# Order of the block products in a row step, packed weights split over two banks at once, and a buffer of its own for the last output block

## The chip, the cores and the metric

The kernel runs on one core of a Trainium2 chip. The metric is the device time of one execution in microseconds (us); a kernel's number is the median of its runs. One further execution was recorded by the hardware profiler, and its times stand in the rows below, counted from the start of its span. PE is TensorE's matmul, PEld its weight load, DVE is VectorE, ACT ScalarE, POOL GpSimd, and SP issues the DMAs.

## The reference, cut to what matters

```python
def reference(q, k, v, p, moe_*, moe2_*):       # B, H, S, D = 8, 8, 576, 64; 32 packed queries
    pp  = softmax(p k^T / 8) v                   # packed attention, per batch and head
    x   = softmax(q pp^T / 8) pp                 # unpacked again: 4608 tokens x 512
    xn  = x / sqrt(mean(x * x) + 1e-6) * rms_g
    y   = (silu(xn w_gate) * (xn w_val)) w_out   # 512 -> 1536 -> 512
    return ((y w1) * (y w2)) w3 w_out2           # 512 -> 1024 -> 1024 -> 512
```

## The kernel before

Each factor of a matrix product is split into a rounded high part and the rest (`split`, line 58: ACT copies to the high part, then an engine subtracts, nearly always DVE, for the low part), and three products (high high, high low, low high) stand for one in full precision.

**Attention and gated layer** (to about 524 us). For batch `b`, `wb_unit(b, g)` (line 335) multiplies the batch's packed values into one sixth `g` of the gate and value weights: 16 small matmuls on PE (line 342) fill a tile `t` of 128 x 2 x 512 that covers two PSUM banks. It is then split into `wbh` and `wbl`, by one ACT and one DVE instruction for each half `e`, four in all; there are 48 such units. `dense_units(b)` (line 367) runs the dense work: groups of six matmuls of 288 columns fill one of four banks (`gv`), first the gate group, which ACT (tanh, line 387, tile `th`) and DVE (line 388) read, then the value group, which ACT reads (line 392, tile `vl`). In a group the order is (wbh, ah), (wbh, al), (wbl, ah), so the low part is first needed by the fifth matmul. `wb_unit` for the next sixth is issued when four groups of the present one are left. The pieces of the attention of later batches are issued between the groups, at places written out by hand, and each engine works through its queue in program order.

**Down projection and weight folding** (to about 862 us). `group` (line 612) also lays out the seven combinations of w1 and w2 for the last part, in the order `ORDER` (line 595).

**Bilinear layers** (from 862 us to the end). Tokens come in five pairs of strips, three pairs of 512 columns and two of 384 (called wide and narrow below). `run(p)` (line 937) makes eight row steps and then a last layer. The products go by a scheme with seven block products for eight. `step(p, n)` (line 863) does the seven products of one row: each is six matmuls, into four banks `ta`, `tb`, `tc_`, `td`, which alternate between two sets from step to step. Before the change the order on PE is 0, 5, 4, 1, 6, 3, 2. Into `ta` go products 0 and then 1, into `tb` 5 and then 6, into `tc_` 4 and then 2, into `td` 3. The second product of a bank is added on top of the first, so it has to wait for whoever still reads the first: ACT reads product 0 (`p1`), DVE reads 5 for `u2`, DVE reads 6 for `u3`, then 4 for `c22`, which needs `u3`. Then DVE makes `s1`, from `td` and `u3`, multiplies it by `ta`, and adds `tc_` to `u2`; POOL does the rest. `u2` and `c22` are the two halves of a tile `uc` with two buffers, `p1` and `u3` come from a tile `hr` with five. The weights come by DMA in two units a step (products at positions 0 to 2, and 3 to 6), through four buffers.

The **last layer** runs 168 matmuls (line 973). `u3` (block 1, 0) and `c22` (block 1, 1) are stored from where they are; block (0, 1) is written over `u2` in `uc` and stored from there. The stores go out on SP's queue, one after each quarter of a product, and what is left at the end of the pass (line 1007).

Of the kernel before, what the change touches and what calls it, by code (L numbers as in the profile page):

```python
# [32 lines left out]
def packed_attention_swiglu_bilinear(ctx: ExitStack, tc, qT, kT, v, pT, rms_g, w_gv, w_out,  # L33
                                     w1, w2, w3T, w_out2, out):
    nc = tc.nc
# [16 lines left out]
    def slot(tag):  # L52
        return slots.tile([128, 2, 512], F32, tag=tag, name=tag, bufs=2)
# [4 lines left out]
    def split(hi, lo, src, eng_lo):  # L58
        nc.scalar.activation(out=hi, in_=src, func=AF.Copy)  # L59
        eng_lo.tensor_tensor(out=lo, in0=src, in1=hi.bitcast(F32), op=ALU.subtract)  # L60
# [274 lines left out]
    def wb_unit(b, g):  # L335
        gP1T = res["gP1T", b]
        while not all((g, c) in converted for c in range(NC)):
            next(gvw)
        t = slot("at")
        for c in range(NC):  # L340
            for e in range(2):
                nc.tensor.matmul(t[32 * c:32 * c + 32, e, :], lhsT=gP1T[64 * e:64 * e + 64, c, :],  # L342
                                 rhs=wgv[64 * e:64 * e + 64, c, :, 256 * g:256 * g + 256],
                                 start=True, stop=True, tile_position=(64 * e, 32 * c), skip_group_check=True)
        hi = dp.tile([128, 2, 512], F32R, tag="wbh", name="wbh", bufs=2)
        lo = dp.tile([128, 2, 512], F32R, tag="wbl", name="wbl", bufs=2)
        for e in range(2):
            split(hi[:, e], lo[:, e], t[:, e], nc.vector)
        wb[b, g] = (hi, lo)


# [56 lines left out]
    def drain(gen):  # L408
        for _ in gen:
            pass  # L410
# [36 lines left out]
    def wb_first():  # L447
        wb_unit(0, 0)
        yield
# [17 lines left out]
    for n in range(16):  # L467
        r, c = GROUPS[n // 4]
        w, kk = ((w1, r), (w1, r + 2), (w2, r), (w2, r + 2))[n % 4]
# [122 lines left out]

    ORDER = (0, 5, 4, 1, 6, 3, 2)
    parts = []

    def fetch_part(n):
# [13 lines left out]
    def group(g):  # L612
# [5 lines left out]
        def put(j, src, eng):  # L618
            hi, lo = (to[:, :, ORDER.index(j), s, :] for s in range(2))
            split(hi, lo, src.rearrange("p (i n) -> p i n", i=4), eng)  # L620
# [153 lines left out]
    def next_w():  # L774
        w = ws.pop(0)
        load_w()
        return w

    def width(p):
        return pairs[p][1]  # L780
# [5 lines left out]
    def diff(out, a, b, eng=None):  # L786
        (eng or nc.vector).tensor_tensor(out=out, in0=a, in1=b, op=ALU.subtract)
# [57 lines left out]
    def banks(n):  # L845
        if n % 2:
            return [pt.tile([128, 512], F32, tag="at", name="at", bufs=4) for _ in range(4)]
        return four("gv")
# [5 lines left out]
    def tmp():  # L854
        return rot.tile([128, TT], F32, tag="hr", name="hr", bufs=5)

    def two():
        return yp.tile([128, 2, TT], F32, tag="y", name="uc", bufs=2)

    def dve(out, a, b, op=ALU.add):  # L860
        nc.vector.tensor_tensor(out=out, in0=a, in1=b, op=op)  # L861

    def step(p, n):
        w = width(p)
        i = LAYER[n]
        half, k = divmod(i, 4)
        xh, xl = xs[p]

        def side(name):
            return sides[name][:, k, :w]  # L870

        def prod(t, j, start):
            pos = ORDER.index(j)
            wi, pos, n = (wa, pos, 3) if pos < 3 else (wb_, pos - 3, 4)
            wi = wi[:, :512 * n].rearrange("p (r j s n) -> p r j s n", r=2, j=n, s=2)
            at = 0
            for a, x in ((0, xh), (1, xh), (0, xl)):
                for r in range(2):
                    nc.tensor.matmul(t, lhsT=wi[:, r, pos, a], rhs=x[:, j, r, :w],  # L879
                                     start=(start and at == 0), stop=(at == 5), skip_group_check=True)  # L880
                    at += 1

        ta, tb, tc_, td = (t[:, :w] for t in banks(n))
        p1, u3, uc = tmp()[:, :w], tmp()[:, :w], two()
        u2, c22 = uc[:, 0, :w], uc[:, 1, :w]
        s1, s2 = (side("s21"), side("s22")) if half else (side("s11"), side("s12"))
        wa = next_w()
        prod(ta, 0, True)
        nc.scalar.activation(out=p1, in_=ta, func=AF.Copy)
        prod(tb, 5, True)  # L890
        dve(u2, tb, p1)
        prod(tc_, 4, True)
        yield
        wb_ = next_w()
        prod(ta, 1, False)
        prod(tb, 6, False)
        dve(u3, tb, p1)
        dve(c22, tc_, u3)
        yield
        prod(td, 3, True)  # L900
        dve(s1, td, u3)
        dve(s1, s1, ta, ALU.mult)
        prod(tc_, 2, False)
        dve(u2, tc_, u2)
        nc.gpsimd.tensor_tensor(out=s2, in0=u2, in1=c22, op=ALU.mult)  # L905
        if half == 0:
            diff(side("t1s"), s2, s1, nc.gpsimd)
        else:
            diff(side("t2s"), s2, side("t1s"), nc.gpsimd)
            diff(side("s12"), s2, side("s12"), nc.gpsimd)  # L910
            diff(side("t4s"), s1, side("t2s"), nc.gpsimd)
        yield
# [24 lines left out]
    def run(p):  # L937
        w = width(p)
        ahead = splitting(p, AHEAD)
        diffs = early(p + 1)  # L940
        for n in range(8):
            for part, _ in enumerate(step(p, n)):
                if part in EARLY.get(n, ()):
                    next(ahead)
                if n == 1 and part == 0:
                    fetch_y(p + 1)
                if n in (4, 5) and part == 1:
                    next(diffs, None)
        xs.pop(p)
        drain(ahead)  # L950
        drain(diffs)
        later = splitting(p, LATER)
        sum_ = sums(p + 1)
        acc = [[t[:, :w] for t in banks(m)] for m in range(2)]
        p1, u2, u3, c22 = [], [], [], []
        out_stores = []

        def keep(m, half, side, o):
            out_stores.append(dict(out=out[256 * half + 128 * m:256 * half + 128 * m + 128,
                                           pairs[p][0] + side * w:pairs[p][0] + side * w + w], in_=o))  # L960

        BANK = {0: 0, 1: 0, 5: 1, 6: 1, 4: 2, 2: 2, 3: 3}
        for a, j in enumerate(PROD):
            wi = next_w().rearrange("p (s i n) -> p s i n", s=2, i=4)
            last = {0: 1, 5: 6, 4: 2}.get(j, j) == j
            for k in range(4):
                for _ in range(ISSUE[4 * a + k]):
                    next(later, None)
                hi, lo = his.pop((j, k))
                for m in range(2):  # L970
                    t = acc[m][BANK[j]]
                    for n, (s, x) in enumerate(((0, hi), (1, hi), (0, lo))):
                        nc.tensor.matmul(t, lhsT=wi[:, s, k, 128 * m:128 * m + 128], rhs=x,  # L973
                                         start=(j in (0, 5, 4, 3) and k == 0 and n == 0),
                                         stop=(k == 3 and n == 2), skip_group_check=True)
                if k == 1:
                    next(sum_, None)
                if out_stores:
                    nc.sync.dma_start(**out_stores.pop(0))
            for m in range(2):  # L980
                ta, tb, tc_, td = acc[m]
                if j == 0:
                    p1.append(tmp()[:, :w])
                    nc.scalar.activation(out=p1[m], in_=ta, func=AF.Copy)
                elif j == 5:
                    uc = two()
                    u2.append(uc[:, 0, :w])
                    c22.append(uc[:, 1, :w])
                    dve(u2[m], tb, p1[m])
                elif j == 1:  # L990
                    c11 = tmp()[:, :w]
                    nc.scalar.activation(out=c11, in_=ta, func=AF.Copy)
                    keep(m, 0, 0, c11)
                elif j == 6:
                    u3.append(tmp()[:, :w])
                    dve(u3[m], tb, p1[m])
                    dve(c22[m], tc_, u3[m])
                    keep(m, 1, 1, c22[m])
                elif j == 3:
                    dve(u3[m], td, u3[m])  # L1000
                    keep(m, 1, 0, u3[m])
                elif j == 2:
                    dve(u2[m], tc_, u2[m])
                    keep(m, 0, 1, u2[m])
        drain(sum_)
        for x in out_stores:
            nc.sync.dma_start(**x)

    for p in range(len(pairs)):
        run(p)  # L1010
# [31 lines left out]
```

## Time and profile before

| | |
|---|---|
| time, median of 3 runs | 1409.88 us (1409.6 to 1412.5) |
| the profiled execution: its own time, and the span in the profile | 1410.05 us, 1408.3 us |
| busy over the span | PE 95%, PEld 79%, DVE 61%, POOL 43%, ACT 41% |
| PE on the chain that ended last | 79% (DVE 10%) |

The chain is followed back from the last instruction, at each step to what released it. A busy PE counts every matmul, also one that runs at a lower granted clock. An idle engine only costs time where the chain passes through it.

### The profile page before, as it was taken

How to read it: one execution, taken by the hardware profiler on the slowest of the kernel's cores; microseconds unless marked ns; L12 is line 12 of the kernel's file. 1: busy time of each engine (PE TensorE's matmuls, PEld its weight loads, DVE VectorE, ACT ScalarE, POOL GpSimd, SP SyncE). 2: the span in 40 equal slices, each digit the busy share in tenths (PEclk: the TensorE clock that was granted, in tenths of full speed). 3: DMA queues.
4: the chain of work that ended last, by engine and by line, in shares of the span. 5: the costliest groups of instructions: out<-in, count | busy, mean ns of one | idle time of the engine just before them, and what ended most of it. 6: DMA issues, size and time to landing. Idle time of an engine off the chain costs nothing.

```text
span 1408.3 us, 23274 instructions
## 1 busy us (share of the span) xinstructions
PE 1339.0 (95%) x8800; PEld 1119.5 (79%) x8800; DVE 857.2 (61%) x1356; ACT 573.7 (41%) x1141; POOL 606.5 (43%) x524
## 2 busy tenths in 40 slices
PE   4579999999999999999999999999999999999998
PEld 2358888788787888888878888778777777899998
DVE  4787776866767556745376564566458357457445
ACT  2455555655655665634243342024015103304113
POOL 2455456465555562312132212446345534535533
PEclk9699999999999999999999999999999999999999
DMA  9763566554542357743299875556655745777775
GB/s 315 280 216 89 214 203 211 186 178 146 175 142 106 128 167 246 266 154 121 83 341 375 341 265 210 214 196 226 256 194 190 275 178 209 244 278 254 265 257 181
DMA packets 86688, 301.94 MB, mean 214 GB/s; under 512 B 9520, under 2 KB 14640, under 8 KB 72624
## 3 DMA queue, kind: packets, MB, share of 16 engines
q1 hardware_dynamic: 86576, 300.46, 61.6%
q8 instruction: 69, 1.13, 0.4%
q14 instruction: 43, 0.35, 0.1%
HBM read 223.87 MB, written 76.55 MB: 213 GB/s over the span
## 4 chain that ended last, share of the span: by engine, by line
PE 79%; DVE 10%; ACT 2%; issue 2%; DMA 1%; POOL 1%; SPq 0%; ACTq 0%; DVEq 0%; POOLq 0%
PE gv L381 17%; PE at L568 12%; PE gv L879 11%; PE at L879 11%; PE gv L568 7%; PE gv L973 6%; PE at L973 6%; PE gv L669 3%; PE at L342 3%; DVE uc L861 2%; DVE hr L861 2%; PE at L297 1%; DVE th L388 1%; DVE c_t L115 1%; DVE wbl L60 1%
## 5 line engine op out<-in xcount | busy, mean ns | idle before, releaser
L393 POOL TENSOR_TENSOR ht<-th,vl 128x288 f32<-128x288 f32 x192 | 162.1, 854 | 118.7 <-ACT vl L392 61.6
L381 PE MATMUL gv<-ah,wbh 128*128 128x288 f32 x768 | 178.3, 313 | 15.8 <-ACT vl L392 11.1
L381 PEld LDWEIGHTS gv<-ah,wbh 128*128 128x128 f32 x768 | 122.0, 190 | 67.8 <-issue 22.8
L381 PE MATMUL gv<-al,wbh 128*128 128x288 f32 x768 | 166.7, 298 | 0.0
L381 PE MATMUL gv<-ah,wbl 128*128 128x288 f32 x768 | 164.7, 296 | 0.0
L905 POOL TENSOR_TENSOR s<-uc 128x512 f32<-128x512 f32 (+1 forms) x40 | 48.9, 1223 | 238.8 <-DVE uc L861 238.8
L60 DVE TENSOR_TENSOR hl<-hr,hh 128x512 fp32r<-128x512 f32 x108 | 99.4, 926 | 77.8 <-ACT hh L59 77.8
L118 POOL TENSOR_TENSOR c_o<-c_o,c_y 128x512 int32<-128x512 int32 x52 | 70.7, 1360 | 172.1 <-DVE c_o L116 111.3
L879 PE MATMUL gv<-xh,w 128*128 128x512 f32 (+1 forms) x560 | 140.6, 372 | 3.4 <-DVE uc L861 2.8
L879 PE MATMUL at<-xh,w 128*128 128x512 f32 (+1 forms) x560 | 140.4, 372 | 3.4 <-DVE uc L861 2.5
L381 PEld LDWEIGHTS gv<-al,wbh 128*128 128x128 f32 x768 | 124.4, 190 | 1.1 <-DVE al L60 1.1
L381 PEld LDWEIGHTS gv<-ah,wbl 128*128 128x128 f32 x768 | 124.2, 189 | 0.0
L879 PEld LDWEIGHTS gv<-xh,w 128*128 128x128 f32 x560 | 101.3, 188 | 24.0 <-DVE uc L861 11.3
L879 PEld LDWEIGHTS at<-xh,w 128*128 128x128 f32 x560 | 101.3, 188 | 23.6 <-DVE uc L861 11.0
L388 DVE SCALAR_TENSOR_TENSOR th<-th,gv 128x288 f32<-128x288 f32 x192 | 84.9, 445 | 50.6 <-ACT th L387 47.1
L59 ACT ACTIVATE hh<-hr 128x512 fp32r<-128x512 f32 x108 | 67.7, 629 | 117.2 <-PE at L568 58.5
L568 PE MATMUL at<-hh,wo_l 128*128 128x512 f32 x288 | 112.1, 389 | 0.0
L568 PE MATMUL at<-hh,wo_h 128*128 128x512 f32 x288 | 112.1, 389 | 0.0
L568 PE MATMUL at<-hl,wo_h 128*128 128x512 f32 x288 | 112.1, 389 | 0.0
L392 ACT ACTIVATE vl<-gv 128x288 f32<-128x288 f32 x192 | 80.0, 417 | 57.6 <-PE gv L381 53.0
L60 DVE TENSOR_TENSOR wbl<-at,wbh 128x512 fp32r<-128x512 f32 x96 | 65.8, 686 | 60.9 <-ACT wbh L59 60.3
L387 ACT ACTIVATE th<-gv 128x288 f32<-128x288 f32 x192 | 79.6, 415 | 35.9 <-PE gv L381 35.8
(154 smaller groups left out, 2815.4 us busy)
## 6 DMA issues: line engine op xcount, KB each, us to landing
w<-ws_d SPq DMA_DIRECT2D x40, 1024.0 KB, 5.0
w<-w_d SPq DMA_DIRECT2D x35, 1024.0 KB, 4.8
w<-ws_d SPq DMA_DIRECT2D x40, 768.0 KB, 5.1
hT_d<-ht SPq DMA_DIRECT2D x96, 288.0 KB, 3.3
hr<-hT_d SPq DMA_DIRECT2D x108, 256.0 KB, 4.6
w<-in_w_gv_dram SPq DMA_DIRECT2D x24, 512.0 KB, 7.0
w<-in_w_out_dram SPq DMA_DIRECT2D x20, 512.0 KB, 4.2
v<-in_v_dram SPq DMA_DIRECT2D x8, 1152.0 KB, 8.1
```

Source lines behind the costliest of these rows:

```text
L59: nc.scalar.activation(out=hi, in_=src, func=AF.Copy)
L60: eng_lo.tensor_tensor(out=lo, in0=src, in1=hi.bitcast(F32), op=ALU.subtract)
L118: nc.gpsimd.tensor_tensor(out=d, in0=d, in1=shape(y), op=ALU.add)
L381: nc.tensor.matmul(t[:, :HALF], lhsT=w[:, e, 256 * i + 128 * f:256 * i + 128 * f + 128], rhs=x[:, e, HALF * hf:HALF * hf + HALF], start=(n ...
L387: nc.scalar.activation(out=th, in_=t[:, :HALF], func=AF.Tanh, scale=0.5)
L388: nc.vector.scalar_tensor_tensor(out=th, in0=th, scalar=1.0, in1=t[:, :HALF], op0=ALU.add, op1=ALU.mult)
L392: nc.scalar.activation(out=vl, in_=t[:, :HALF], func=AF.Copy, scale=0.5)
L393: nc.gpsimd.tensor_tensor(out=ht[:, hf], in0=th, in1=vl, op=ALU.mult)
L568: nc.tensor.matmul(acc[m], lhsT=w[:, kk, 128 * m:128 * m + 128], rhs=x, start=(kk == 0 and a == 0), stop=(kk == NF - 1 and a == 2))
L861: nc.vector.tensor_tensor(out=out, in0=a, in1=b, op=op)
L879: nc.tensor.matmul(t, lhsT=wi[:, r, pos, a], rhs=x[:, j, r, :w], start=(start and at == 0), stop=(at == 5), skip_group_check=True)
L973: nc.tensor.matmul(t, lhsT=wi[:, s, k, 128 * m:128 * m + 128], rhs=x, start=(j in (0, 5, 4, 3) and k == 0 and n == 0), stop=(k == 3 and n ...
```

## The change

Three edits.

- In `step`, product 6 comes before product 1 on PE, and the weights lie in that order (`ORDER`). The order on DVE stays u2, u3, c22, s1, s1, u2.
- In `wb_unit` the tile of two banks is split by one ACT instruction and one DVE instruction of 1024 elements a partition each, where there were two of 512 on either engine.
- In the last layer block (0, 1) is written to a buffer of the tile `hr` and stored from there, no longer from `u2`'s half of `uc`.

```diff
@@ wb_unit
         lo = dp.tile([128, 2, 512], F32R, tag="wbl", name="wbl", bufs=2)
-        for e in range(2):
-            split(hi[:, e], lo[:, e], t[:, e], nc.vector)
+        split(hi, lo, t, nc.vector)
@@
-    ORDER = (0, 5, 4, 1, 6, 3, 2)
+    ORDER = (0, 5, 4, 6, 1, 3, 2)
@@ step
         wb_ = next_w()
-        prod(ta, 1, False)
         prod(tb, 6, False)
         dve(u3, tb, p1)
         dve(c22, tc_, u3)
+        prod(ta, 1, False)
         yield
@@ run, last layer
                 elif j == 2:
-                    dve(u2[m], tc_, u2[m])
-                    keep(m, 0, 1, u2[m])
+                    c12 = tmp()[:, :w]
+                    dve(c12, tc_, u2[m])
+                    keep(m, 0, 1, c12)
```

## Rows read from the trace of the kernel before

**Rows 1.** The page, part 1: busy us (share of the span) x instructions.

```profile
PE 1339.0 (95%) x8800; PEld 1119.5 (79%) x8800; DVE 857.2 (61%) x1356; ACT 573.7 (41%) x1141; POOL 606.5 (43%) x524
```

**Rows 2.** Busy time by stretch: us, PE, PEld, DVE, ACT, POOL, granted clock, DMA.

```profile
0.00:110.00 110.00, 63.17 (x666) 43.37 (x667) 77.51 (x138) 50.05 (x99) 46.68 (x49) 0.83 0.75 262
110.00:475.00 365.00, 353.86 (x3736) 296.79 (x3734) 256.91 (x512) 210.53 (x493) 201.13 (x220) 1.00 0.49 163
475.00:524.00 49.00, 49.00 (x403) 43.09 (x396) 27.05 (x48) 33.26 (x79) 30.76 (x32) 1.00 0.52 165
524.00:862.40 338.40, 337.51 (x1488) 278.88 (x1487) 195.98 (x241) 145.25 (x241) 79.63 (x48) 1.00 0.67 236
862.40:942.40 80.00, 78.80 (x338) 62.46 (x337) 40.13 (x56) 9.34 (x16) 29.33 (x21) 1.00 0.64 230
1220.30:1282.50 62.20, 60.61 (x338) 58.06 (x337) 30.26 (x56) 6.41 (x14) 21.05 (x20) 1.00 0.80 283
```

**Rows 3.** The chain in order of time, one wide row step: start us, us, what.

```profile
882.50 6.83 PE gv L879 x30
...
890.08 0.70 DVE uc L861
...
890.83 1.67 PE gv L879 x6
892.50 0.69 PE at L879 x3
```

**Rows 4.** The chain in order of time, one narrow row step.

```profile
1266.98 5.22 PE gv L879 x30
...
1274.77 1.39 PE at L879 x8
```

**Rows 5.** Timeline of DVE, u2 of a wide and two narrow steps [idle before, releaser].

```profile
885.38 0.69 DVE L861 TENSOR_TENSOR uc<-gv,hr 128x512 f32<-128x512 f32 x1 [2.15 <-PE gv L879]
...
1269.21 0.56 DVE L861 TENSOR_TENSOR uc<-gv,hr 128x384 f32<-128x384 f32 x1 [1.21 <-POOL s L905]
...
1277.34 0.56 DVE L861 TENSOR_TENSOR uc<-at,hr 128x384 f32<-128x384 f32 x1 [1.97 <-ACT sh L59]
```

**Rows 6.** Timeline of SP and DVE around the start of the last pass.

```profile
1308.42 0.95 SPq L979 DMA_DIRECT2D out_dram<-hr  x2
...
1316.14 0.56 DVE L861 TENSOR_TENSOR uc<-gv,hr 128x384 f32<-128x384 f32 x1 [3.00 <-DMA out_dram<-uc]
```

**Rows 7.** Waits, 110 to 475 us: total us, times, longest us.

```profile
ACT wbh L59 <- DVE wbl L60: 40.1, 38, 2.3
...
PE gv L381 <- ACT vl L392: 10.9, 8, 2.1
```

**Rows 8.** Groups by line, 110 to 524 us: busy us, mean ns of one, idle before.

```profile
L388 DVE SCALAR_TENSOR_TENSOR th<-th,gv 128x288 f32<-128x288 f32 x180 | 79.7, 446 | 49.2 <-ACT th L387 45.8 <-POOL ht L393 2.3 <-POOL rinv L315 0.8
L387 ACT ACTIVATE th<-gv 128x288 f32<-128x288 f32 x179 | 74.2, 415 | 35.6 <-PE gv L381 35.5
L60 DVE TENSOR_TENSOR wbl<-at,wbh 128x512 fp32r<-128x512 f32 x88 | 60.4, 686 | 58.2 <-ACT wbh L59 57.6
L59 ACT ACTIVATE wbh<-at 128x512 fp32r<-128x512 f32 x88 | 52.7, 599 | 61.2 <-DVE wbl L60 45.1 <-PE at L342 15.9
```

**Rows 9.** Timelines of ACT, DVE and PE, one stall of the gated layer.

```profile
209.30 0.64 ACT L59 ACTIVATE wbh<-at 128x512 fp32r<-128x512 f32 x1
212.25 0.60 ACT L59 ACTIVATE wbh<-at 128x512 fp32r<-128x512 f32 x1 [2.31 <-DVE wbl L60]
...
211.59 0.63 DVE L60 TENSOR_TENSOR wbl<-at,wbh 128x512 fp32r<-128x512 f32 x1
212.88 0.69 DVE L60 TENSOR_TENSOR wbl<-at,wbh 128x512 fp32r<-128x512 f32 x1 [0.66 <-ACT wbh L59]
...
213.51 0.53 PE L381 MATMUL gv<-ah,wbh 128*128 128x288 f32 x2 [2.05 <-ACT vl L392]
```

**Rows 10.** Timeline of PE, a stall of the start-up.

```profile
106.85 0.85 PE L381 MATMUL gv<-ah,wbh 128*128 128x288 f32 x2 [2.32 <-DVE th L388]
```

## Prediction

> **What bounds the kernel now.** First the page: PE is busy for 95% of the span [rows 1], so what can still be won is mostly idle time of PE, about 70 us, and the question is where it lies and who ends it. The table by stretches answers the first half [rows 2]. Of the idle time 46.8 us lie in the first 110 us (start-up, clock 0.83), 11.1 us between 110 and 475 us (the gated layer), none between 475 and 524 us, under 1 us in the down projection, and then a little in each set of eight row steps: 1.2 us of 80 in a wide pass, 1.6 us of 62.2 in a narrow one. A busy PE is modelled, so in the row steps I don't trust that last figure but time the steps by the chain.
>
> The chain of a wide step [rows 3]: 30 matmuls run from 882.50 for 6.83 us, 0.228 us each. They are products 0, 5, 4, 1, 6. Then the chain leaves PE for DVE, which makes u3 and c22 one after the other (c22 ends at 890.78), and comes back at 890.83 for the last six, product 2. Product 3 runs meanwhile, but it lasts only 1.37 us, and two DVE instructions of 0.70 us and their latencies last 1.50. The next step starts at 892.50: 10.00 us for 42 matmuls that at the pace of the first thirty would take 42 x 0.2277 = 9.56. So 0.44 us a step is lost: part of it idle, part the cold start of product 2. A narrow step [rows 4] goes from 1266.98 to 1274.77, 7.79 us against 42 x 0.174 = 7.31: 0.48 there, and 0.46 over the eight steps (62.2 / 8 = 7.77, [rows 2]).
>
> In the gated layer the waits [rows 7] put all of PE's own 10.9 us on eight waits for ACT's `vl`. And ACT itself waits 40.1 us, 38 times, for DVE's `wbl` before a `wbh`. There are 38 units in that stretch: the second half of the split waits for DVE's first half every time, though it reads another bank. One stall shows the link [rows 9]: ACT ends the first half of wbh at 209.94, then sits for 2.31 us, because DVE, behind on other work, comes to the first wbl only at 211.59. The second wbh starts at 212.25, tanh and `vl` stand behind it, and PE, idle since 211.46, goes on at 213.51.
>
> **The order of products.** No instruction is added. Product 1 (1.37 us wide, 1.04 narrow) moves from before product 6 to after it. u3 and c22 then have products 1 and 3 to hide behind, 2.73 us wide and 2.09 narrow, and need 1.50 us wide and about 1.2 narrow (two instructions of 0.56 [rows 5] and 0.05). The wait of product 2 goes, and 0.44 or 0.46 us a step with it: 24 x 0.44 + 16 x 0.46 = 17.9 us.
>
> What is late next is product 6. It adds onto `tb`, so it waits until u2 has read product 5. Before, products 4 and 1 covered that, now only 4. Wide: the step starts at 882.50, product 5 ends 2.73 us in, u2 runs from 885.38 to 886.07 [rows 5], 3.57 us in; product 6 would start 4.10 us in. Cover 0.5 us. Narrow: u2 ends at 1269.77, 2.79 us in, against 3.13: cover 0.34, of which the weight load ahead of the matmul takes about 0.2. So it just fits. In the eighth step of the first narrow pass u2 ends at 1277.90 [rows 5], 3.13 us after 1274.77: there product 6 would be late by 0.1 to 0.3. I take 0.3 us for such cases; the bound is 0.2 us in all 16 narrow steps, 3.2 us. On DVE u2 heads the queue of the step; behind it stand a low part of the split in five of eight steps, u3 and c22, which have over 1 us to spare. s1 needs product 3, which keeps its place as sixth, and `ta`, now a product earlier than that. The weights' two units hold the same products as before, so DMA loads and their buffers don't move; DMA is 80% busy in a narrow pass, and a step 6% shorter makes it 85%.
>
> Term: -17.9 + 0.3 = -17.6, bounds -14.5 and -18.
>
> **The last block's own buffers.** Without this edit the new order would pay at each pass's start: u2 of a pass's first step waits for the store out of `uc`, 3.00 us in the last pass [rows 6], so that it ends at 1316.70, where product 6 in its new place could start 3.13 us after the step's start at 1312.55, at 1315.68: 1 us there, and 0.5 at the other narrow start. With it u2 waits only for the store of c22, issued two products (over 8 us) earlier. The cost moves to `hr`: two tiles more a pass, so u3 of the first step gets the buffer from which the last layer's u3 was stored. That store is issued at 1308.42 [rows 6], and u3 comes due at about 1317; the two stores before it from `uc` were free well within 8 us. No wait, and the DVE instruction itself is as long as before. Term: 0 by itself; the cover of the first term.
>
> **The split over two banks.** Neither long form is in the trace from this tile. DVE: 446 ns for 288 elements and 686 for 512 [rows 8] give 1.07 ns an element over a fixed 137, so 1235 for 1024; two took 1372. ACT: 415 for 288 and 599 for 512 give 0.82 and 178, so 1020; two took 1198. As a chain before: 0.60 + 0.69 + 0.60 + 0.69 and three hand-overs of 0.05 or so, about 2.75 us, and ACT blocked until the second half is out; after: 1.02 + 1.24, 2.3 us, and ACT free after 1.02 whatever DVE does. The high part of the first half comes 0.4 us later than before, but its first reader stands four groups (3.3 us) behind.
>
> The stall at 211.46 again: ACT would be done at 210.35, tanh and `vl` would follow at once, and the bank would be free before PE asks. Then the low part decides: DVE gets to it at 211.59 and ends at 212.83. It is wanted by the fifth matmul, at about 212.0. The stall falls from 2.05 to 0.85; and as the same edit frees DVE 0.3 to 0.8 us earlier at the two units before it on that chain, I take 0.6. Of the eight stalls, 10.9 us in all and the longest 2.1 [rows 7], four are of this size: 1.45 x 4 = 5.8 won. The other four share about 2.9 us; three of them, 2.4 us in all, have the second wbh just before them in the same way, and go. Sum -8.2; bounds nothing (if another backlog of ACT and DVE holds the banks) and -10.9, all there is [rows 7].
>
> In the start-up four more units run, with PE idle 2.32 us behind one of them for DVE's tanh product [rows 10], which waits on DVE's queue behind the second wbl. Each such place wins 0.4 to 0.8 us; I take -2, bounds 0 and -5 (a shorter idle could also spare a stretch at the lower clock: those matmuls at 106.85 run at half pace). Between 475 and 524 us PE has no idle time [rows 2], so the units there win nothing.
>
> One page speaks against this edit. The row: the second half starts only after DVE has finished with the first, 38 times in 38 [rows 7]. The Trainium skill, in PSUM — Partial Sum Buffer (section Specifications (TRN2)), says that ScalarE and VectorE can read PSUM in parallel at full bandwidth as long as they don't collide in a bank. By it the halves would overlap, 0.60 + 0.69 + 0.69 = 2.0 us against 2.3, and the merged form would lose. The trace shows no such overlap here, so the sum goes by the rows.
>
> **Sum.** -17.6 - 8.2 - 2 = -27.8. From the profiled execution's own time, 1410.05: 1382.2, say 1382. The median of the runs is 0.2 lower, which is nothing. Ends: 1410 - 14.5 = 1395.5 and 1410 - 18 - 10.9 - 5 = 1376.
>
> **Rivals.**
> 1. The split wins almost nothing: ACT and DVE have a backlog in the stalls anyway (the chain there runs through reductions and conversions on DVE too). Against it: ACT is seen waiting, 2.31 us, not working. 1410 - 17.6 - 1 = 1391.
> 2. The narrow steps keep part of their loss: u2's cover there is thin. 0.2 us in 16 steps: 1382 + 3 = 1385; if product 6 starts cold as well, 0.35 us: 1388.
> 3. The loss only moves: product 6 waits for u2 as long as product 2 did for c22, and only the split gains: 1410 - 11 = 1399. Against it: cover is there in every row of u2 that I read.
> 4. Slower: u2 falls behind the split's low part or the sums for the next pass on DVE (1.2 us at most places), so that product 6 is 0.8 us late and product 1 is no cover any more. In 40 steps +32 - 17.9 - 11 = +3: 1413. It decides from about 0.7 us of delay a step. Against it: u2 stands first in the step's part of the queue, and DVE idles 1.2 to 2.2 us before it [rows 5].
> 5. The halves did overlap where it mattered, so the merged split loses 0.3 us at each of the eight stalls and four units of the start-up: 1410 - 17.6 + 3.6 = 1396.
>
> **How the numbers follow.** Forecast (1376 to 1388, with rival 2 within it) 0.76; rival 1 0.13; rival 3 0.04; rival 5 0.03; rival 4 0.03; no change 0.01. A difference under 0.2% (2.8 us) can't be told from none. All but rival 4 and no change are faster by more: faster 0.95, same 0.02, slower 0.03. The range 1375 to 1396 takes in the bounds of each term and rivals 1 and 5.
>
> **What would show it.** Wide steps of 9.56 to 9.6 us and narrow ones of 7.3 to 7.4; no wait of PE for `uc` before product 2. One wbh of about 1.02 and one wbl of 1.24 us a unit; ACT's wait for `wbl` gone; PE's waits for `vl` between 110 and 475 us down from 10.9 us to about 2. The prediction is wrong if product 6 waits for `uc` in most steps, if PE still idles for about 2 us at a time behind `vl` in the gated layer, or if the first step of a pass waits for a store out of `hr`.

## The result and the profile after

The changed kernel takes 1374.06 us (1373.85 to 1374.66, 4 runs) against 1410.26 us: a ratio of 0.974, 95% interval 0.972 to 0.976. The forecast was 1382 us with a range from 1375 to 1396; the direction and the mechanisms were right, and the gain of 36 us was larger than forecast: the time lies 0.9 us below the range. The profiled execution took 1373.85 us, 36.2 less than that of before.

Busy time by stretch of the changed kernel, in the columns of [rows 2] and with the stretches moved to the same work: start-up, two parts of the gated layer, down projection, the steps of a wide and of a narrow pass.

```profile
0.00:110.00 110.00, 64.56 (x688) 43.79 (x688) 78.80 (x136) 50.43 (x98) 47.34 (x50) 0.80 0.76 262
110.00:475.00 365.00, 362.21 (x3844) 306.76 (x3845) 257.16 (x484) 220.76 (x475) 210.68 (x227) 1.00 0.51 170
475.00:507.00 32.00, 32.00 (x264) 28.95 (x263) 19.18 (x29) 22.91 (x51) 22.27 (x24) 1.00 0.53 167
507.00:845.40 338.40, 337.76 (x1489) 279.19 (x1488) 196.66 (x242) 145.47 (x241) 79.77 (x49) 1.00 0.67 236
845.40:921.50 76.10, 76.10 (x338) 62.95 (x337) 41.22 (x56) 9.35 (x16) 29.37 (x21) 1.00 0.67 242
1192.00:1250.30 58.30, 58.30 (x337) 58.15 (x337) 30.05 (x56) 6.41 (x14) 21.07 (x20) 1.00 0.84 301
```

A wide pass's eight steps fit into 76.1 us with PE busy throughout, where 80.0 were needed. A narrow pass's fit into about 58.4; the stretch of 58.3 shown here has the weight loads busy for 58.15 of them. The gated layer's long stretch keeps 2.8 us of idle PE, of 11.1.

The chain in order of time, a wide and a narrow step (compare [rows 3, 4]):

```profile
864.50 9.52 PE gv L878 x42
874.02 9.52 PE at L878 x42
...
1206.58 7.31 PE gv L878 x42
```

The chain does not leave PE any more: one piece of 42 matmuls a step, where it went over DVE for u3 and c22 after the thirtieth.

The new instructions of the split (groups by line, 110 to 524 us) and all that PE waited for between 110 and 475 us:

```profile
L60 DVE TENSOR_TENSOR wbl<-at,wbh 128x1024 fp32r<-128x1024 f32 x44 | 53.5, 1215 | 42.1 <-ACT wbh L59 42.1
L59 ACT ACTIVATE wbh<-at 128x1024 fp32r<-128x1024 f32 x44 | 45.1, 1024 | 16.1 <-PE at L342 15.8
```
```profile
PE gv L380 <- DVE wbl L60: 1.8, 4, 0.8
PE at L342 <- DVE sq L300: 1.1, 1, 1.1
```

1.02 us for the high part and 1.22 for the low one, as worked out (1.02 and 1.24). ACT no longer waits for `wbl` at all, and of PE's waits for `vl` one of 0.11 us is left; the eight waits of 10.9 us [rows 7] have become four for the low part, 1.8 us.

The same place as in [rows 9], one batch later (timelines of ACT, DVE and PE):

```profile
259.83 1.05 ACT L59 ACTIVATE wbh<-at 128x1024 fp32r<-128x1024 f32 x1
260.73 0.44 ACT L386 ACTIVATE th<-gv 128x288 f32<-128x288 f32 x1
...
262.11 1.16 DVE L60 TENSOR_TENSOR wbl<-at,wbh 128x1024 fp32r<-128x1024 f32 x1
...
262.29 0.43 PE L380 MATMUL gv<-ah,wbh 128*128 128x288 f32 x2
...
263.32 0.53 PE L380 MATMUL gv<-ah,wbl 128*128 128x288 f32 x2 [0.34 <-DVE wbl L60]
```

DVE is late here too, because of its other work: it comes to the low part 1.2 us after the high part is out, against 1.65 in [rows 9]. But ACT goes straight on to tanh at 260.73, without DVE, the bank is free, PE starts the next sixth, and is held only at the fifth matmul, by the low part: the chain that the prediction set out for this stall, with 0.34 us of it left idle.

**Where the 36 us came from**, by the first matmul of each part in the two traces (row steps: from the first matmul of a pass's steps to the first of its last layer, summed over five passes):

| | before | after | change |
|---|---|---|---|
| start-up, to the product with v after 110 us (line 213) | 118.14 | 115.09 | -3.1 |
| from there to the down projection | 405.38 | 391.66 | -13.7 |
| row steps | 364.53 | 345.34 | -19.2 |
| all the rest (difference to the execution's own time) | | | -0.2 |

### The profile page after: what moved, and what is told of

Read it like the earlier page. It is cut to its first block, busy times and chain, and to the rows that moved or that the text cites. A ratio compares the mean times of both kernels' runs of the same rounds, so it can differ in the third digit from the quotient of the medians.

```text
span 1372.1 us, 23271 instructions
## 1 busy us (share of the span) xinstructions
PE 1319.5 (96%) x8800; PEld 1118.3 (82%) x8800; DVE 854.9 (62%) x1308; ACT 574.3 (42%) x1093; POOL 608.0 (44%) x524
## 3 DMA queue, kind: packets, MB, share of 16 engines
HBM read 223.87 MB, written 76.55 MB: 219 GB/s over the span
## 4 chain that ended last, share of the span: by engine, by line
PE 87%; DVE 5%; issue 1%; DMA 1%; POOL 1%; ACT 1%; SPq 0%; ACTq 0%; DVEq 0%; POOLq 0%
PE gv L380 20%; PE gv L878 13%; PE at L878 13%; PE at L567 12%; PE gv L567 7%; PE gv L972 6%; PE at L972 6%; PE gv L668 3%; PE at L342 3%; PE at L297 1%; DVE wgv L116 1%; PE at L213 1%; DMA hr<-hT_d 1%; DVE wbl L60 1%; PE at L309 1%
## 5 line engine op out<-in xcount | busy, mean ns | idle before, releaser
L380 PE MATMUL gv<-ah,wbh 128*128 128x288 f32 x768 | 175.2, 309 | 2.4 <-ACT vl L391 2.0
L878 PE MATMUL gv<-xh,w 128*128 128x512 f32 (+1 forms) x560 | 137.7, 367 | 0.0
L60 POOL TENSOR_TENSOR xl<-yi,xh 128x1024 fp32r<-128x1024 f32 (+1 forms) x20 | 52.1, 2607 | 74.3 <-ACT xh L59 50.8
```

Of the source, the lines that this page charges most:

```text
L380: nc.tensor.matmul(t[:, :HALF], lhsT=w[:, e, 256 * i + 128 * f:256 * i + 128 * f + 128], rhs=x[:, e, HALF * hf:HALF * hf + HALF], start=(n ...
```

## The experiments

All stand against runs of the kernel before on the same chip. Edits are shown against the changed kernel or the one before, as said.

**The three edits one by one** (against the kernel before). New order alone:

```diff
-    ORDER = (0, 5, 4, 1, 6, 3, 2)
+    ORDER = (0, 5, 4, 6, 1, 3, 2)
...
-        prod(ta, 1, False)
         prod(tb, 6, False)
         dve(u3, tb, p1)
         dve(c22, tc_, u3)
+        prod(ta, 1, False)
```

> The new order of products alone, with the old split and the last block still stored from u2's half of uc. Theory (the three gains are separate, and the order is worth what the row steps got shorter): in the changed kernel eight wide steps take 76.2 us instead of 80.0 and eight narrow ones 58.4 instead of 62.3, 19.3 us in all; without the block's own buffers the first step of a pass loses about 1.0 us in the last pass and 0.5 in the first narrow one, so -17.8, about 1392.4. Rival (the gains hang together, PE in the row steps is fast only because something else came earlier): less than -12, over 1398.

The new order and the block's own buffer (in addition `c12 = tmp()`, as in the change):

> The new order and the last block's own buffer, with the old split. Theory: -19.3, about 1391, and all eight steps of every pass alike. If the own buffer does nothing for the order, the same as with the order alone within 0.3 us.

The split alone:

```diff
-        for e in range(2):
-            split(hi[:, e], lo[:, e], t[:, e], nc.vector)
+        split(hi, lo, t, nc.vector)
```

> The split over two banks alone. Theory: the bilinear part begins 17.1 us earlier as in the changed kernel (845.4 instead of 862.5 us), and nothing else moves: 1393.2. Rival (my recorded term of -10.2 was right, and the rest came with the other edits): 1400.

The block's own buffer alone:

```diff
-                    dve(u2[m], tc_, u2[m])
-                    keep(m, 0, 1, u2[m])
+                    c12 = tmp()[:, :w]
+                    dve(c12, tc_, u2[m])
+                    keep(m, 0, 1, c12)
```

> The last block's own buffer alone, with the old order. Theory: u2 of a pass's first step no longer waits for a store, but product 6 comes late enough in the old order, so no difference but the 0.3 to 0.4 us of the last pass's first step: 1409.9 to 1410.3. Rival (the store out of uc held PE already before): -1.5 or more.

| kernel | time, us | ratio, 95% interval | down projection starts | row steps |
|---|---|---|---|---|
| order alone | 1396.53 | 0.988 to 0.992 | 526.50 | 348.75 |
| order and block | 1391.52 | 0.985 to 0.988 | 523.15 | 345.54 |
| split alone | 1392.92 | 0.986 to 0.989 | 506.59 | 364.70 |
| block alone | 1409.43 | 0.999 to 1.001 | 524.72 | 363.80 |

The order with its buffer wins 19.0 us in the row steps and nothing ahead of them; the split wins 16.9 us ahead of them (523.52 to 506.59) and nothing in them. 19.0 + 16.9 = 35.9: the two are separate and add up. The rivals that tied them together fall.

The order alone missed its number (1392.4 expected). One part is the store out of `uc`. In the last pass (DVE's timeline of that kernel):

```profile
1302.19 0.56 DVE L861 TENSOR_TENSOR uc<-at,uc 128x384 f32<-128x384 f32 x1
1306.02 0.56 DVE L861 TENSOR_TENSOR uc<-gv,hr 128x384 f32<-128x384 f32 x1 [3.27 <-DMA out_dram<-uc]
```

u2 ends at 1306.58, product 6 follows at 1306.64, and the narrow passes' steps take 1.2 us (0.3 of it in the last step) and 1.6 us more than with the buffer, the two wide ones after the first 0.25 to 0.3. That makes 3.4 us by single steps and 3.2 by the table (348.75 - 345.54, as one wide step of the run with the buffer lasted 0.17 us longer than the others), where 1.5 were reckoned. In the last step of the first narrow pass u2 waits for ACT and not for a store; with the buffer this wait is gone as well, and why is not shown. The buffer by itself, in the old order, wins nothing that can be measured. The profiled execution of that kernel took 1397.16 us; the other 3 us of its miss lie ahead of the part that the edit touches: the down projection begins at 526.50 in that execution, and at 523.15 to 524.72 in three others with the same code up to there.

**What the split's gain is** (against the changed kernel). Both high halves first, as instructions of 512:

```diff
-        split(hi, lo, t, nc.vector)
+        for e in range(2):
+            nc.scalar.activation(out=hi[:, e], in_=t[:, e], func=AF.Copy)
+        for e in range(2):
+            nc.vector.tensor_tensor(out=lo[:, e], in0=t[:, e], in1=hi[:, e].bitcast(F32), op=ALU.subtract)
```

> The changed kernel, but the split of the packed weights is four instructions again, both high halves first, then both low halves. ACT then waits for no low half, while all fixed costs of the shorter instructions are back (about 0.18 us on ACT and 0.14 on DVE a unit, 48 units). Theory A (the gain of the split is ACT no longer waiting for DVE in the middle of a unit): 1374 to 1377. Theory B (the gain is the fixed cost of two instructions a unit, 48 x 0.32 = 15 us): 1389 or so.

1375.29 us (ratio 0.974 to 0.977), down projection at 506.92. The fixed costs of 96 more instructions are back, and it costs about 1 us, which the intervals don't even separate. So theory A: the gain is that ACT does not wait for DVE in the middle of a unit.

Why did it wait, if the second half reads another bank? A tile of its own for each half, in the old order high, low, high, low:

```diff
-        hi = dp.tile([128, 2, 512], F32R, tag="wbh", name="wbh", bufs=2)
+        hi = [dp.tile([128, 512], F32R, tag=f"wbh{e}", name=f"wbh{e}", bufs=2) for e in range(2)]
...  # lo in the same way
-        split(hi, lo, t, nc.vector)
+        for e in range(2):
+            split(hi[e], lo[e], t[:, e], nc.vector)
```

> The changed kernel, but the split is four instructions in the old order (high, low, high, low), with a tile of its own for each half of wbh and wbl; the PSUM tile of two banks is as before. If the second high half waited because both halves lay in one tile of wbh, it now starts while DVE still reads the other bank, and ACT is free 1.25 us after the start whatever DVE does: 1374 to 1376. If it waited because both read one PSUM tile of two banks, the wait for the first low half stays and the time is that with the old split, about 1391.

1391.03 us (0.986 to 0.989): the whole gain of the split is gone. Its waits, 110 to 475 us:

```profile
ACT wbh L59 <- DVE wbl L60: 40.0, 38, 2.3
...
PE gv L381 <- ACT vl L392: 10.7, 8, 2.0
```

They are those of the kernel before [rows 7]. So a tile of its own for each half of `wbh` does not take the wait away. The same tiles, highs first:

> As the kernel with tiles of their own for the halves, but both high halves are issued before both low halves. The first low half needs only the first high half, so if the two engines may read the two banks at the same time the unit lasts 0.60 + 0.69 + 0.69 = 2.0 us instead of 2.3, and stalls that end with a low half end 0.3 us earlier: 1373 to 1374. If the banks can't be read at the same time, as with the highs first in one tile.

1375.11 us (0.974 to 0.977), no better than with one tile. ACT and DVE in one unit:

```profile
130.53 1.09 ACT L348 ACTIVATE wbh<-at 128x512 fp32r<-128x512 f32 x2 [0.92 <-PE at L342]
...
131.65 1.29 DVE L350 TENSOR_TENSOR wbl<-at,wbh 128x512 fp32r<-128x512 f32 x2 [0.58 <-ACT wbh L348]
```

The first low half starts only when the second high half is out, at 131.62, so the hoped-for overlap did not come. Last, a PSUM tile of its own for each half, in the order high, low, high, low (against the kernel with own tiles in that order):

```diff
-        t = slot("at")
+        t = [slot("at") for _ in range(2)]
...
-            split(hi[e], lo[e], t[:, e], nc.vector)
+            split(hi[e], lo[e], t[e][:, 0], nc.vector)
```

> As the kernel with tiles of their own for the halves of wbh and wbl, in the order high, low, high, low, and in addition each half comes from a PSUM tile of its own (the first bank of each of the two two-bank tiles). If the shared PSUM tile made ACT's second high half wait for DVE's first low half, the waits of wbh for wbl (38 times, 40 us between 110 and 475 us) go, and the second high half follows the first at once, while DVE reads the other bank in its usual 0.69 us. If the engines can't read two banks at once, or the wait has another cause, they stay. The time itself says little: each unit now takes both PSUM tiles that the attention works with, so PE may wait for those; between 1374 and 1400.

1386.11 us (0.980 to 0.986). ACT and DVE in one unit, and PE's waits between 110 and 475 us:

```profile
133.18 1.08 ACT L59 ACTIVATE wbh<-at 128x512 fp32r<-128x512 f32 x2 [2.75 <-PE at L342]
...
133.81 1.29 DVE L60 TENSOR_TENSOR wbl<-at,wbh 128x512 fp32r<-128x512 f32 x2 [1.93 <-ACT wbh L59]
```
```profile
PE at L342 <- DVE bdG L244: 5.1, 6, 0.9
PE gv L381 <- DVE wbl L60: 0.3, 2, 0.2
```

ACT's two high halves now follow each other, 133.18 to 134.26, and DVE reads the first bank from 133.81, while ACT still reads the second. ACT's waits for `wbl` (40.0 us, 38 times) are gone from the list. The unit takes 1.92 us, where the two long instructions take about 2.3. This kernel differs from the one that waits only in the PSUM tiles, so it was the shared PSUM tile that put the wait between the two engines there, and the two banks can be read at once. Whether it would do with `wbh` in one tile was not run. The kernel is slower than the changed one, and the down projection begins at 517.10, 10.35 us later. Each unit takes both PSUM tiles, and PE now waits for those: 5.1 us of idle time are seen, and the rest was not placed. Own tiles without that price were not tried.

**How thin u2's cover is** (against the changed kernel). Product 6 right after product 5:

```diff
-    ORDER = (0, 5, 4, 6, 1, 3, 2)
+    ORDER = (0, 5, 6, 4, 1, 3, 2)
...
         dve(u2, tb, p1)
+        prod(tb, 6, False)
+        yield
+        wb_ = next_w()
+        dve(u3, tb, p1)
         prod(tc_, 4, True)
-        yield
-        wb_ = next_w()
-        prod(tb, 6, False)
-        dve(u3, tb, p1)
         dve(c22, tc_, u3)
```

> The changed kernel, but product 6 comes right after product 5, before product 4, so that nothing on PE covers u2. Theory (product 6 waits for u2 and a cold start): in a wide step u2 ends 1.05 us after product 5 and the restart costs 0.1: 1.1 us a step; narrow 0.3 + 0.56 + 0.05 + 0.1 = 1.0 us; 40 steps, 24 x 1.1 + 16 x 1.0 = 42 us: 1416. u3 and c22 still have products 4, 1 and 3 around them. If the cover were not needed: 1374.

1418.64 us (1.005 to 1.008), slower than before any change. The chain:

```profile
867.45 2.73 PE gv L878 x12
...
870.31 0.70 DVE uc L860
...
871.05 7.14 PE gv L878 x30
878.19 2.73 PE at L878 x12
```

A step is 10.74 us: products 0 and 5, then u2 on the chain, then the other thirty. Over all 40 steps 389.58 - 345.34 = 44.2 us, 1.1 a step, close to the 42 reckoned. Product 4 is worth that much where it stands.

u2 a little late, by a DVE copy of 64 or 256 columns ahead of it:

```diff
+        nc.vector.tensor_copy(idle[:, :64], tb[:, :64])      # or 256
         dve(u2, tb, p1)
```

> The changed kernel, with a DVE copy of 64 columns of tb into a spare tile ahead of u2 in every step (about 0.2 us, its source is product 5, so u2 is later by that much). It adds 40 small instructions that nothing reads. The prediction gave u2 a cover of 0.5 us in wide steps and 0.34 in narrow ones, of which the weight load takes about 0.2. If that is right wide steps stay at 9.52 us, and narrow ones grow by 0 to 0.1: 1374 to 1376. If the whole 0.34 is free, nothing moves.

> The same with a copy of 256 columns (about 0.4 us). Wide: 0.4 of 0.5 us of cover, at most 0.1 us a step late once the weight load counts. Narrow: 0.1 us over the cover, and with weight load and cold start 0.2 to 0.3 us a step: 16 x 0.25 = 4 us, 1378. If u2 had no thin cover but over a microsecond, nothing moves.

With 64 columns 1374.61 us (0.973 to 0.976): a wide step stays at 9.52, a narrow one grows by 0.03. With 256 columns 1379.04 us (0.976 to 0.979): wide +0.05 a step (76.55 to 76.59 a pass), narrow +0.20 (60.03 instead of 58.40). The copies take 0.225 and 0.425 us each, and the longer one puts u2 off by 0.34, as DVE's timeline in a narrow step shows:

```profile
1203.45 0.42 DVE L891 COPY idle<-at 128x256 f32<-128x256 f32 x1 [1.51 <-PE at L879]
1203.79 0.55 DVE L861 TENSOR_TENSOR uc<-at,hr 128x384 f32<-128x384 f32 x1
```

Of 0.34 us of delay a narrow step pays 0.20 and a wide one 0.05: free cover of about 0.15 and 0.3 us. That agrees with u2's end less the weight load (0.34 - 0.2, as the prediction had it, and 0.5 - 0.2); that the weight load is what takes the difference was not tested.

u2 behind the split's low part:

```diff
-        dve(u2, tb, p1)
         prod(tc_, 4, True)
         yield
+        dve(u2, tb, p1)
```

> The changed kernel, but u2 is issued after the low part of the split that the step's first break brings (four breaks in eight steps), so that DVE does that first. This is rival 4 of the prediction made real in those steps. In a wide pass the low part lasts 0.7 to 1.8 us from about 2.2 us after the step's start, u2 then ends at 3.7 to 4.8 us and product 6 is late by up to 0.8; narrow 0.6 to 1.0 us. 20 steps x 0.4 = 8 us: 1382, and steps without a break stay at 9.52 and 7.31.

1392.25 us (0.985 to 0.988), 18 us over the changed kernel where 8 were expected. In a step with such a break (timeline of DVE and PE):

```profile
867.63 1.47 DVE L60 TENSOR_TENSOR sl<-s,sh 128x512 fp32r<-128x512 f32 x1 [1.82 <-ACT sh L59]
869.03 0.68 DVE L860 TENSOR_TENSOR uc<-gv,hr 128x512 f32<-128x512 f32 x1
...
869.76 1.19 PE L878 MATMUL gv<-xh,w 128*128 128x512 f32 x4 [0.60 <-DVE uc L860]
```

The low part waits for its high part until 867.63, and u2 ends at 869.71. That costs 0.9 us in each of the 20 steps concerned: rival 4's mechanism, at half its places, takes back nearly all that the new order won.

## Why the prediction was right or wrong

**The order of products: right, 1.6 us too small.** -17.6 was forecast with -18 as the far end; -19.2 came, and 19.0 with the order and its buffer alone. The wait of product 2 went whole, and product 6 waits nowhere: PE waits for nothing in all 40 steps. The term was mis-sized by the pace: thirty matmuls in 6.83 us carry some of the step's ends in them, and 42 in a row take 9.52 us, not 9.56, which is 1 us over 24 steps. The last narrow pass had more to lose than the one I timed, and the 0.3 us set aside for u2 were not needed (without the block's own buffer they were: see the order alone). The far end left no room for any of this.

**u2's cover: right in size.** Forecast at 0.5 and 0.34 us, less 0.2 for the weight load; the late copies gave about 0.3 and 0.15. Rivals 2, 3 and 4 did not happen: narrow steps take 7.31 us, with no wait left. With no cover the steps are 25 us slower than before the change (389.58 against 364.53), and with u2 second in DVE's queue in half of them 1.3 us faster (363.19).

**The block's own buffer: right in kind, too small.** As the cover of the new order it is worth 3.2 us, not 1.5: the store out of `uc` also touched the wide passes, which I had counted as covered (0.25 to 0.3 us each), and the narrow ones more than I had it. Its price on `hr` was nothing, as forecast.

**The split: mechanism right, and the step that failed.** -8.2 was forecast for the gated layer, and -10.9 named as "all there is". It won 13.7. The 10.9 were the idle time of PE, and the sum treated that as the price of the stalls. It isn't. The chain around a stall of the kernel before, 0.50 us of idle time at 436 us:

```profile
433.95 2.38 PE gv L381 x18
...
436.83 1.06 PE gv L381 x6
```

Eighteen matmuls take 2.38 us, 0.79 for six; six after a wait take 1.06, all of it booked as busy. So a stall costs 0.27 us on top of its idle time. Taken from start to start of the matmuls, it is 0.26 or 0.27 at each of the eight stalls before, and at each of the five that are left (four for the low part, one of 0.11 us for `vl`).

Between the two marks of the table above PE runs the same 4064 matmuls in the same order in both kernels, so the 13.7 us can be told apart. 9.0 are idle time (11.1 to 2.1), and 4.7 are time in which the profile shows PE as busy (394.4 to 389.7). Of these 4.7, the restarts are 0.8, as there are three fewer. The other 3.9 lie at places without a stall, where the next matmul starts up to 0.11 us sooner than before; together they are worth more than the restarts. One of these places, before and after (timelines of PE):

```profile
136.93 0.54 PE L381 MATMUL gv<-ah,wbh 128*128 128x288 f32 x2
137.30 0.61 PE L381 MATMUL gv<-al,wbh 128*128 128x288 f32 x2
...
133.80 0.43 PE L380 MATMUL gv<-ah,wbh 128*128 128x288 f32 x2
134.07 0.42 PE L380 MATMUL gv<-al,wbh 128*128 128x288 f32 x2
```

Two matmuls end 0.1 to 0.2 us later than their pace, with no idle time in front; at the second of these places a weight load waits 0.15 us for DVE's `al`. 0.7 of the 3.9 us lie between the unit at 474.24 and the down projection at 523.52, where PE showed no idle time and I forecast no gain: the same work now runs from 458.19 to 506.75. What held the matmuls at the other places stays open. In the row steps I had seen that the busy figure hides time, and priced by the chain. In the gated layer I did not.

That is also how the time left the range: its far end added 18, 10.9 and 5 us, and 19.2, 13.7 and 3.1 came. Without the gated layer's 2.8 us beyond "all there is", the time would have been inside it.

**What is left of a large stall** was forecast at 0.6 us, decided by the low part. It was 0.45 (1.8 us in four), and by the low part. Rival 1 (the backlog would keep the banks) falls.

**Start-up: right.** -2 with bounds 0 and -5; -3.1 in the profiles. In five profiles in which ACT waits for DVE as before it ends at 116.6 to 119.0 us, in eight with ACT freed at 114.4 to 115.4.

**The rule on two banks.** To go by the trace's 38 waits of 38 was right for the sum: no overlap was there to lose, and rival 5 falls. But the waits were the kernel's own, from sharing one PSUM tile; with a PSUM tile for each half the two engines do overlap (1.92 us a unit, and two instructions take 1.08 us on ACT and 1.29 on DVE, against 1.09 and 1.29 one engine after the other). The Trainium skill (PSUM — Partial Sum Buffer, section Specifications (TRN2)) says that ScalarE and VectorE can access PSUM in parallel as long as they don't collide in a bank. That run agrees with it.

## What to carry to other kernels

Price a stall from the chain, by the distance between the same two instructions with and without it, and not from the idle column: a matmul run that restarts after a wait costs more than the gap shows (0.27 us here), matmuls can also come late without any gap, and idle time is then no upper bound for a gain. When two engines take turns on one tile that covers several PSUM banks, look whether the second engine has to wait at all; one long instruction on each engine, or all of the first engine's work ahead of the second's, frees the first engine for what is queued behind it. Before moving a product earlier, add up what still covers the reader of its bank: here 0.15 us of cover were enough, and with none the row steps were 25 us slower than before the change instead of 19 faster.

## What the runs showed of the hardware that was not expected

Six 288-column matmuls take 1.06 us after a wait and 0.79 in a run, at a granted clock of 1.00 in both. In narrow steps back to back the weight loads are busy for 58.15 of 58.30 us, and the pace (7.31 us for 42) was no slower than within the thirty of before. The part ahead of the down projection varies between executions of one and the same code: in four with the old split the down projection began between 523.15 and 526.50 us, in eight with ACT freed (six of them the same code up to there) between 506.55 and 507.87.
